# When the loads of one unit may start: a fixed time on the plan's clock, or the landing of a weight quarter

## The chip, the cores and the metric

The kernel runs on one core of one Trainium2 chip. The metric is the device time of one execution in microseconds (us). A core has five engines that run side by side, each through its own list of instructions in order: TensorE (PE in the profile; its weight loads are PEld), VectorE (DVE), ScalarE (ACT), GpSimd (POOL) and SyncE (SP). DMA transfers are started from SP's list (queue q1, "hardware_dynamic") or from POOL's (queue q0, "software_dynamic", which also casts fp32 to bf16 on the way) and run on 16 DMA engines that both queues share.

## What is computed

The inputs are q, k and v of shape (8 batches, 8 heads, 576 positions, 64), w_in (512 x 2048) and w_out (2048 x 512). First a retention layer, then a feed-forward layer over its 4608 rows of 512 (the reference, shortened):

```python
scores = scale * np.matmul(q, k.transpose(0, 1, 3, 2))
Dmat = np.where(rel >= 0, gamma[:, None, None] ** rel[None, :, :], 0.0)
attn = np.matmul(scores * Dmat[None], v)
x = attn.transpose(0, 2, 1, 3).reshape(B * S, H * D)
h = x @ w_in
g = np.where(h > 0.0, h, np.exp(np.minimum(h, 0.0)) - 1.0)
out = g @ w_out
```

rel is the distance of two positions, gamma one factor for each head.

## The kernel before

The retention is cut into items: a batch and one of its two stretches T of 256 positions, plus the items X and Y for the last 64 positions of four batches each. The six items of batches 0 to 2 are cut again, into two units of four heads each, so units 0 to 11 (u0 to u11): u0 and u1 make item 0, u2 and u3 item 1, u4 and u5 item 2. For each unit, three loads of 256 KB bring its q, k and v as fp32 from DRAM. DVE or POOL scale q and k by powers of gamma (line 522), ACT or POOL cast v (532), PE transposes q and k (554; from unit 6 on a DMA does it, 543), ACT or DVE copy them out of PSUM (560). Then PE makes scores, DVE masks them (888), PE makes the state and the values (line 265 is the helper of all matmuls, so they are told apart by tiles), DVE and others add up the state (823, 825, 841), and ACT or DVE write the result to xt, the input of the feed-forward layer (924).

The feed-forward layer goes by blocks. Blocks 0 to 13 are 256 rows wide, one item each; block 0 needs u0 and u1, block 1 u2 and u3, block 2 u4 and u5. F1 is the first layer: for 16 pieces of 128 columns of w_in, four matmuls of 128x256 each; two pieces share a PSUM bank, so F1 of such a block is eight groups of eight matmuls. After each group ACT takes the exponential (1041), ACT or DVE do a second step (1051, 1053, 1055), DVE makes g (1063, 1065). F2 is the second layer: each tile of 128 rows takes 16 matmuls of 128x512, four for each quarter of w_out. Block 0's F2 goes by pieces of w_out over its two tiles, all others go tile by tile.

The weights arrive in parts, started from POOL: w_in as wi0 and wi1 (one eighth each, 256 KB in bf16) and wi2, wi3, wi4 (a quarter each, 512 KB); w_out as wo0 to wo3 (a quarter each, 512 KB). The constants W_IN and W_OUT (lines 223, 224) name the parts.

The order in which each engine does all this is not written out by hand. A planner in the kernel (class Plan, lines 36 to 191) runs through the program as it is built, with a cost in microseconds for each step, ranks, slots of buffers, and a small model of the two DMA queues: ENTER and SW_ENTER are the times from issue to a transfer's first byte, the pair given as dma is its length and its number of packets, LEAVE the time from last byte to landing. At each moment each engine takes the ready step of lowest rank. What comes out is an order for each engine; on the chip there is no clock in it, only that order and the semaphores of true dependences. Where the plan shows PE a gap before 50 us, the code at lines 1183 to 1195 fills 0.8 of it with matmuls or transposes of a tile of zeros.

Four means shape the start of the order:

- AT (line 216) gives the earliest planned time at which a weight part may be issued on POOL (rank -1000, so first of what is ready).
- All loads are issued by SP in one chain, in the order in which `load` names them (378). For the items in VLATE (215) both units' v come after both units' q and k.
- HOLD (214) names loads that get an instruction on POOL ahead of them, planned not before the given time: a memset of one column of the load's tile (383). Because the load overwrites that tile, SP has to wait for the memset. All loads behind it in the chain are held with it.
- `cost_of` (933) and the numbers in `flush` (1019) tell the plan what PE's attention steps cost.

Of the kernel before, what the change touches and what calls it, by code (L numbers as in the profile page):

```python
# [191 lines left out]


ENTER, LEAVE = 1.25, 0.55
SW_ENTER = 4.2
TR_SP = 4.6
SLACK = 3.6
KV = 1.4
ISSUE = 0.65
JOINT = True  # L200
BD_ACT = 0.6
BD_POOL = 0.46
UB_POOL = 0.33
SCALED = 1.06
# [6 lines left out]
EARLY = 6  # L211
PE_TURN = 6
APART = (4, 5)
HOLD = {"ldq4": 14.4, "ldq5": 23.9, "ldv4": 30.1, "ldv6": 24.3}
VLATE = (0,)
AT = {"wi0": 6.9, "wi1": 10.0, "wi2": 7.2, "wi3": 11.0, "wi4": 17.7, "wo0": 18.0, "wo1": 21.0, "wo2": 21.3, "wo3": 27.5}
RANKS = {}
FREE = ("f", "e", "em", "g", "ot")
SURE = 3
# [13 lines left out]
def kernel(  # L233
# [28 lines left out]
    pin = tc.keep_in_program_order  # L262
# [113 lines left out]
    def load_part(name, dst, src, key, first, shape, cost=(0.9, 32)):  # L376
        def emit(op):
            pin(nc.sync.dma_start(dst(), src))  # L378

        hold = None  # L380
        if first and name in HOLD:
            def emit_h(op):
                pin(alu[op.eng].memset(tiles[key][:, 0, :1], 0.0))

            hold = add(f"hold{name}", {"POOL": 0.1}, [], emit_h, len(plan.ops) - 1000, take=[T("r", key, shape, FP32)])
            hold.early = HOLD[name]
            first = False
        op = add(name, {"SP": ISSUE}, [hold], emit, len(plan.ops), take=[T("r", key, shape, FP32)] if first else [],
                 use=[] if first else [key], dma=cost, after=chain.get(0))
        chain[0] = op  # L390
        return op

    def runs(src, b, hs, T):
        return src[b, hs, TB * T : TB * (T + 1), :].rearrange("h (p e) d -> p h (e d)", e=2)

    def load(it):
        n = it.n
        shape = [P, 2 * H, D]
        if it.units:
            for u, what in [(u, what) for u in it.units for what in "qkv"] if it.n not in VLATE else \  # L400
                    [(u, what) for u in it.units for what in "qk"] + [(u, "v") for u in it.units]:
                hs = slice(4 * u.w, 4 * u.w + 4)
                if what == "q":
                    u.ld = {}
                if what == "v":
                    u.ld["v"] = load_part(
                        f"ldv{u.n}", lambda hs=hs: tiles["rv", n].rearrange("p (h e) d -> p h (e d)", e=2)[:, hs],
                        runs(v, it.b, hs, it.T), ("rv", n), u.w == 0, shape, (0.89, 32))
                    continue
                i = "qk".index(what)  # L410
                u.ld[what] = load_part(
                    f"ld{what}{u.n}",
                    lambda u=u, i=i: tiles["rqk", u.n].rearrange("p (h e) d -> p h (e d)", e=2)[:, 4 * i : 4 * i + 4],
                    runs((q, k)[i], it.b, hs, it.T), ("rqk", u.n), i == 0, shape, (0.89 if u.n or not i else 1.5, 32))
            return
        it.ld = {}
        for name, src in (("v", v), ("k", k), ("q", q)):
            key = ("r" + name, n)
            it.ld[name] = []

            def part(tag, lo, n, s, b, t, key=key, src=src, name=name):
                def dst():
                    if s is None:
                        return tiles[key][lo : lo + n].rearrange("p (h e) d -> p h (e d)", e=2)
                    return tiles[key][lo : lo + n, s * H : (s + 1) * H]

                def rows_in():
                    if s is None:
                        return src[b, :, t : t + 2 * n, :].rearrange("h (p e) d -> p h (e d)", e=2)
                    return src[b, :, t : t + n, :].rearrange("h p d -> p h d")  # L430

                it.ld[name].append(load_part(f"ld{name}{tag}_{it.n}", dst, rows_in(), key, not it.ld[name], shape,
                                             ((1.8 if s is None else KV) * n / P, 64 * n // P)))

            if not it.tail:
                t = TB * it.T
                for s in (None,) if name == "q" else range(2):
                    part("" if s is None else s, 0, P, s, it.b, t + P * (s or 0))
            elif name == "q":
                for c in range(NC):  # L440
                    part(c, c * R, R, None, it.b + c, 2 * TB)
            else:
                for s in range(2):
                    for par in range(2):
                        part(2 * s + par, par * C, C, s, it.b + 2 * s + par, 2 * TB)
# [3 lines left out]
    def load_w_in(i):  # L449
        n0, n1 = W_IN[i]  # L450
        c = slice(n0 * 256, n1 * 256)

        def emit(op):
            pin(nc.gpsimd.dma_start(w_in_sb[:, :, c], moe_w_in[:, c].rearrange("(j p) n -> p j n", p=P)))

        op = add(f"wi{i}", {"POOL": 0.8}, [], emit, -1000, dma=(1.92 if n1 - n0 == 1 else 1.43 * (n1 - n0), 32 if n1 - n0 == 1 else 16 * (n1 - n0), SW_ENTER))
        op.slack = 0.4
        for ft in range(2 * n0, 2 * n1):
            w_in_ld[ft] = op

    def load_w_out(i):
        n0, n1 = W_OUT[i]

        def emit(op):
            pin(nc.gpsimd.dma_start(w_out_sb[:, 4 * n0 : 4 * n1],  # L465
                                    moe_w_out[n0 * 512 : n1 * 512, :].rearrange("(f p) n -> p f n", p=P)))

        op = add(f"wo{i}", {"POOL": 0.8}, [], emit, -1000, dma=(2.75 * (n1 - n0), 32 * (n1 - n0), SW_ENTER))
        op.slack = 0.4
        for ft in range(4 * n0, 4 * n1):  # L470
            w_out_ld[ft] = op
# [234 lines left out]
    def ustate_of(u, c):  # L706
        return ("s", u.b, 2 * u.T + c, u.w) if u.T + c else None
# [194 lines left out]
    def state_keys(it):  # L902
        return [s for s in ([ustate_of(it, c) for c in range(2)] if it.unit else [state_of(it, c) for c in range(NC)]) if s]
# [28 lines left out]

    def cost_of(it, parts):
        if it.unit:
            return (0.112 if state_keys(it) and "i" in parts else 0) + 0.24 * sum(p in parts for p in "sv") + \
                0.13 * ("t" in parts)
        t = 0.32 if "i" in parts else 0.0
        return t + 0.26 * sum(p in parts for p in "svt")

    def reserve(op, keys):  # L940
# [72 lines left out]
    def flush(it):  # L1013
        xkey = ("x", it)

        def emit(op):
            attend(it, None, xkey, None, 0)

        iv = add(f"iv{order_of.index(it)}", {"PE": (0.22 if it.unit and ustate_of(it, 0) is None else 0.45) + cost_of(it, "iv")}, inter_deps(it), emit, it.rank + 2, use=inter_uses(it))
        reserve(iv, pair_of(xkey))  # L1020
        put_x(it, xkey, iv)

# [207 lines left out]
```

## Time and profile before

| | before |
|---|---|
| median of 3 runs | 303.13 us |
| lowest and highest | 302.92 and 303.5 us |
| the profiled execution, its time | 302.48 us |
| the profiled execution, its span of instructions | 300.8 us |
| PE busy in the span | 294.7 us (98%) |
| DMA bytes moved | 50.41 MB |
| software queue q0, MB | 4.19 |

The page of the profile gives busy times by engine, slices of the span, DMA queues, the chain of work that ended last, and the costliest groups of instructions. Further views are answers to questions on the same trace: the timeline (start, length, engine, line, operation, output <- input, count, and in square brackets the idle time ahead and what ended it), the windows (busy time of each engine in a stretch, on request of one tile's instructions alone), the DMA view of a narrow window (each issue with its KB and its microseconds from issue to landing; the bytes of each queue in the window), and the chain in order of time. Matmul times in a row overlap: eight matmuls of 0.27 each start about 0.11 apart.

### The profile page before, as it was taken

The page shows a single profiled execution, that of the slowest core. Times are in us where ns is not written, and L with a number is a line of the kernel's source. Part 1 is how long each engine was busy: PE and PEld are TensorE (multiplying, and loading weights), DVE is VectorE, ACT ScalarE, POOL GpSimd, SP SyncE. Part 2 cuts the span into 40 slices and gives each one's busy share as a digit, 9 for nine tenths or more (in the row PEclk, how much of TensorE's full clock was granted, in tenths as well). Part 3 has the DMA queues.
Part 4 walks back from the last instruction along what each step waited for, and adds up shares of the span by engine and source line. Part 5 has one row for each costly group of instructions (what it writes and reads, how often), then busy time and mean ns, then how long its engine had stood idle before and what let it go on. Part 6 is the DMA issues. An engine that isn't in the chain of part 4 may idle for free.

```text
span 300.8 us, 9242 instructions
## 1 busy us (share of the span) xinstructions
PE 294.7 (98%) x3851; PEld 191.2 (64%) x3851; DVE 199.2 (66%) x379; ACT 164.5 (55%) x307; POOL 118.0 (39%) x195
## 2 busy tenths in 40 slices
PE   8999999999999999999999999999999999999995
PEld 5778746758665767677666576767676544444444
DVE  4876924957773777768687567678876667766500
ACT  3658823747653567457456356666666438644311
POOL 5856078654563516348066170835710000000000
PEclk9999999999999999999999999999999999999999
DMA  7999999999999985699999689757231000011131
GB/s 210 270 210 211 229 261 285 211 265 187 287 196 186 298 192 143 183 246 215 253 260 217 162 210 233 189 131 188 57 90 40 35 35 35 2 35 36 44 98 70
DMA packets 123498, 50.41 MB, mean 168 GB/s; under 512 B 83392, under 2 KB 118976, under 8 KB 123456
## 3 DMA queue, kind: packets, MB, share of 16 engines
q1 hardware_dynamic: 118704, 45.63, 64.1%
q0 software_dynamic: 4752, 4.19, 8.6%
q8 instruction: 30, 0.49, 0.7%
q14 instruction: 12, 0.10, 0.1%
HBM read 36.70 MB, written 9.44 MB: 153 GB/s over the span
## 4 chain that ended last, share of the span: by engine, by line
PE 90%; DMA 6%; POOL 2%; issue 0%; DVE 0%; ACT 0%; SPq 0%; ACTq 0%; POOLq 0%
PE f L265 88%; DMA r<-in_k_dram 4%; DMA r<-in_v_dram 3%; PE f L1191 1%; PE f L554 1%; POOL st L522 0%; POOL w_out_sb L465 0%; POOL vn L532 0%; POOL mask L494 0%; POOL pos_i L486 0%; ACT ot L1102 0%; SPq L378 0%; POOL s L841 0%; DVE mid L825 0%; POOL pos_i L489 0%
## 5 line engine op out<-in xcount | busy, mean ns | idle before, releaser
L265 PE MATMUL f<-w_out_sb,g 128*128 128x512 bf16 (+1 forms) x592 | 139.9, 374 | 0.0
L265 PE MATMUL f<-xt,w_in_sb 128*128 128x256 bf16 (+1 forms) x1024 | 139.6, 286 | 0.0
L1041 ACT ACTIVATE e<-f 128x512 f32<-128x512 f32 x144 | 85.6, 597 | 71.9 <-PE f L265 68.1
L265 PEld LDWEIGHTS <-w_in_sb 128*128 128x128 bf16 x1024 | 99.2, 98 | 35.5
L265 PEld LDWEIGHTS <-g 128*128 128x128 bf16 x592 | 56.5, 98 | 52.3
L1055 DVE TENSOR_SCALAR em<-e 128x512 bf16<-128x512 f32 x84 | 42.0, 502 | 40.1 <-ACT e L1041 39.7
L1065 DVE SCALAR_TENSOR_TENSOR g<-f,em 128x512 bf16<-128x512 f32 x84 | 57.0, 688 | 4.8
L1063 DVE SCALAR_TENSOR_TENSOR g<-e,f 128x512 bf16<-128x512 f32 x60 | 40.2, 683 | 10.1 <-ACT f L1051 9.1
L579 POOL CAST kv<-r 128x512 bf16<-128x512 f32 x24 | 14.4, 622 | 59.2 <-issue 57.4
L1102 ACT COPY ot<-f 128x512 f32<-128x512 f32 (+1 forms) x37 | 21.3, 575 | 27.0 <-PE f L265 26.5
L1051 ACT ACTIVATE f<-f 128x512 f32<-128x512 f32 x57 | 33.3, 591 | 0.0
L924 ACT CAST xt<-f 128x512 bf16<-128x512 f32 (+1 forms) x39 | 21.7, 611 | 18.0 <-PE f L265 17.8
L599 POOL TENSOR_TENSOR kv<-r,gk 128x512 bf16<-128x512 f32 x24 | 25.1, 1052 | 5.0 <-DMA r<-in_k_dram 5.0
L599 POOL TENSOR_TENSOR kv<-r,gq 128x512 bf16<-128x512 f32 x24 | 26.1, 1106 | 1.4 <-DMA r<-in_q_dram 1.4
L892 DVE TENSOR_TENSOR pt<-f,mask 128x512 bf16<-128x512 f32 x24 | 15.4, 683 | 9.4 <-PE f L265 9.4
L888 DVE TENSOR_TENSOR pt<-f,mask_u 128x512 bf16<-128x512 f32 x24 | 15.5, 682 | 3.7 <-PE f L265 3.7
L522 POOL TENSOR_TENSOR st<-r,gk 128x256 bf16<-128x256 f32 x21 | 13.1, 640 | 6.9 <-DMA r<-in_k_dram 6.9
L877 POOL CAST bd<-S 128x256 bf16<-128x256 f32 x29 | 11.5, 422 | 9.6 <-DVE S L865 5.9
L865 DVE TENSOR_TENSOR S<-f,S 128x256 f32<-128x256 f32 x30 | 12.6, 421 | 1.9
L522 POOL TENSOR_TENSOR st<-r,gq 128x256 bf16<-128x256 f32 x19 | 11.9, 643 | 1.6 <-DMA r<-in_q_dram 1.2
L265 PE MATMUL f<-T 64*64 64x64 bf16 (+1 forms) x576 | 10.5, 202 | 0.8 <-issue 0.8
L265 PEld LDWEIGHTS <-kv 64*64 64x64 bf16 x704 | 9.5, 104 | 0.1
(64 smaller groups left out, 144.1 us busy)
## 6 DMA issues: line engine op xcount, KB each, us to landing
r<-in_k_dram SPq DMA_DIRECT2D x32, 256.0 KB, 4.6
r<-in_v_dram SPq DMA_DIRECT2D x32, 256.0 KB, 4.9
out_dram<-ot SPq DMA_DIRECT2D x31, 256.0 KB, 2.6
r<-in_q_dram SPq DMA_DIRECT2D x10, 512.0 KB, 5.1
r<-in_q_dram SPq DMA_DIRECT2D x12, 256.0 KB, 5.1
w_out_sb<-in_moe_w_out_dram POOLq DMA_DIRECT2D x4, 512.0 KB, 13.0
w_in_sb<-in_moe_w_in_dram POOLq DMA_DIRECT2D x3, 512.0 KB, 12.1
out_dram<-ot SPq DMA_DIRECT2D x10, 128.0 KB, 2.3
```

Of the source, the lines that this page charges most:

```text
L265: return pin(nc.tensor.matmul(*a, **kw))
L522: pin(alu[op.eng].tensor_tensor(tiles[key][:, i, e].rearrange("p (y x) d -> p x y d", y=2), raw.rearrange("p (x y) d -> p x y d", y=2), g, ...
L599: pin(alu[op.eng].tensor_tensor(tiles[nkey][:, 2 * i + j].rearrange("p (y x d) -> p x y d", y=2, x=HP), raw.rearrange("p (x y) d -> p x y ...
L888: pin(nc.vector.tensor_tensor(pt, src.rearrange("p (h n) -> p h n", h=2), mask_u.rearrange("p k e r -> p (k e r)").unsqueeze(1).to_broadca ...
L892: pin(nc.vector.tensor_tensor(pt.rearrange("p h s n -> p (h s) n"), src.rearrange("p (h n) -> p h n", n=C), mask.rearrange("p e r -> p (e ...
L924: pin(copy[op.eng](dst, src))
L1041: pin(nc.scalar.activation(tiles[ekey], tiles[hkey], AF.Exp))
L1051: pin(nc.scalar.activation(ph, ph, AF.Relu))
L1055: pin(alu[op.eng].tensor_scalar_add(em, e, -1.0))
L1063: pin(nc.vector.scalar_tensor_tensor(g, e, -1.0, ph, ALU.add, ALU.min))
L1065: pin(nc.vector.scalar_tensor_tensor(g, ph, 0.0, tiles[mkey], ALU.max, ALU.min))
L1102: pin(copy[op.eng](tiles[okey][:, :width], tiles[pkey][:, :width]))
```

## The change

Only constants and the way of holding change. First, ldq4 (q of unit 4) alone keeps a hold, and it is no longer a planned time: HOLD now gives it a number of a part of w_out. The instruction ahead of the load is a copy of one column of that part of w_out_sb into the load's tile, on POOL, planned behind the landing of wo1. The loads ldq5, ldv4 and ldv6 lose their holds. Second, VLATE also takes item 1, so its loads go q, k of u2, q, k of u3, then v of both. Third, the times in AT: wi0 is planned later (8.5 for 6.9), wi1 sooner, wi2 later, wi4 and all of w_out sooner. Fourth, the plan's figures: SW_ENTER 3.2 for 4.2; a unit's load 0.84 for 0.89 (the first k 1.4 for 1.5); a part of w_in 1.65 or 1.3 per 256 columns for 1.92 or 1.43; a quarter of w_out 2.6 for 2.75; PE's costs of inter-chunk steps.

```diff
-SW_ENTER = 4.2
+SW_ENTER = 3.2
...
+WI, WI1, LD = 1.3, 1.65, 0.84
...
-HOLD = {"ldq4": 14.4, "ldq5": 23.9, "ldv4": 30.1, "ldv6": 24.3}
-VLATE = (0,)
-AT = {"wi0": 6.9, "wi1": 10.0, "wi2": 7.2, "wi3": 11.0, "wi4": 17.7, "wo0": 18.0, "wo1": 21.0, "wo2": 21.3, "wo3": 27.5}
+HOLD = {"ldq4": 1}
+VLATE = (0, 1)
+AT = {"wi0": 8.5, "wi1": 9.1, "wi2": 8.7, "wi3": 11.8, "wi4": 15.0, "wo0": 15.9, "wo1": 18.0, "wo2": 18.9, "wo3": 25.0}
...
         if first and name in HOLD:
+            behind = HOLD[name]
+
             def emit_h(op):
-                pin(alu[op.eng].memset(tiles[key][:, 0, :1], 0.0))
+                one = tiles[key][:, 0, :1]
+                if isinstance(behind, int):
+                    pin(copy[op.eng](one, w_out_sb[:, 4 * W_OUT[behind][0], :1]))
+                else:
+                    pin(alu[op.eng].memset(one, 0.0))
 
             hold = add(f"hold{name}", {"POOL": 0.1}, [], emit_h, len(plan.ops) - 1000, take=[T("r", key, shape, FP32)])
-            hold.early = HOLD[name]
+            if isinstance(behind, int):
+                holds.append((hold, f"wo{behind}"))
+            else:
+                hold.early = behind
             first = False
...
-                        runs(v, it.b, hs, it.T), ("rv", n), u.w == 0, shape, (0.89, 32))
+                        runs(v, it.b, hs, it.T), ("rv", n), u.w == 0, shape, (LD, 32))
...
-                    runs((q, k)[i], it.b, hs, it.T), ("rqk", u.n), i == 0, shape, (0.89 if u.n or not i else 1.5, 32))
+                    runs((q, k)[i], it.b, hs, it.T), ("rqk", u.n), i == 0, shape, (LD if u.n or not i else 1.4, 32))
...
-        op = add(f"wi{i}", {"POOL": 0.8}, [], emit, -1000, dma=(1.92 if n1 - n0 == 1 else 1.43 * (n1 - n0), 32 if n1 - n0 == 1 else 16 * (n1 - n0), SW_ENTER))
+        op = add(f"wi{i}", {"POOL": 0.8}, [], emit, -1000, dma=(WI1 if n1 - n0 == 1 else WI * (n1 - n0), 32 if n1 - n0 == 1 else 16 * (n1 - n0), SW_ENTER))
...
-        op = add(f"wo{i}", {"POOL": 0.8}, [], emit, -1000, dma=(2.75 * (n1 - n0), 32 * (n1 - n0), SW_ENTER))
+        op = add(f"wo{i}", {"POOL": 0.8}, [], emit, -1000, dma=(2 * WI * (n1 - n0), 32 * (n1 - n0), SW_ENTER))
...
-            return (0.112 if state_keys(it) and "i" in parts else 0) + 0.24 * sum(p in parts for p in "sv") + \
+            return (0.056 if state_keys(it) and "i" in parts else 0) + 0.24 * sum(p in parts for p in "sv") + \
                 0.13 * ("t" in parts)
-        t = 0.32 if "i" in parts else 0.0
+        t = 0.07 * len(state_keys(it)) if "i" in parts else 0.0
...
-        iv = add(f"iv{order_of.index(it)}", {"PE": (0.22 if it.unit and ustate_of(it, 0) is None else 0.45) + cost_of(it, "iv")}, inter_deps(it), emit, it.rank + 2, use=inter_uses(it))
+        iv = add(f"iv{order_of.index(it)}", {"PE": (0.28 if it.unit and ustate_of(it, 0) is None else 0.5) + cost_of(it, "iv")}, inter_deps(it), emit, it.rank + 2, use=inter_uses(it))
```

The list `holds` was there before, empty: at line 1164 each of its pairs gives the hold a dependence on the named weight part.

## The prediction

> **What bounds the kernel now.** I read the page first: span, engines, and the chain that ended last.
>
> ```profile
> span 300.8 us, 9242 instructions
> PE 294.7 (98%) x3851; PEld 191.2 (64%) x3851; DVE 199.2 (66%) x379; ACT 164.5 (55%) x307; POOL 118.0 (39%) x195
> PE 90%; DMA 6%; POOL 2%; issue 0%; DVE 0%; ACT 0%; SPq 0%; ACTq 0%; POOLq 0%
> ```
>
> PE is busy 98% of the span and is 90% of the chain. So the end moves only if PE does its real work sooner, and "busy" has to be split into real work and the zero matmuls that only fill planned gaps. The next two answers are the windows view kept to one tile each (window, its length, PE busy and count): first the tile of zeros, then w_in_sb, which is the first layer, F1.
>
> ```profile
> 14.00:18.00 4.00, 0.93 (x14) 0.68 (x14) 0.00 (x0) 1.00 1.28 204
> 18.00:22.00 4.00, 1.54 (x22) 1.17 (x22) 0.00 (x0) 1.00 1.21 215
> 22.00:26.00 4.00, 0.39 (x4) 0.31 (x4) 0.00 (x0) 1.00 1.21 217
> ```
>
> ```profile
> 14.00:18.00 4.00, 1.04 (x8) 0.74 (x8) 0.81 (x1) 1.00 1.28 204
> 18.00:22.00 4.00, 2.08 (x16) 1.44 (x16) 0.00 (x0) 1.00 1.21 215
> 22.00:26.00 4.00, 3.75 (x32) 3.00 (x33) 0.00 (x0) 1.00 1.21 217
> ```
>
> The columns are window, length, busy time and count of PE and of its weight loads, a third engine (DVE, then POOL), clock, DMA share and GB/s. From 14 to 22 us PE runs 36 matmuls of zeros, from 22 to 26 only four. F1 gets 24 matmuls in those eight microseconds and 32 in the next four. So PE can still win between 14 and 23 us; behind that it has real work nearly all the time. The timeline of PE there and behind, and one row of ACT, the last write of block 1's input:
>
> ```profile
> 15.98 1.04 PE L265 MATMUL f<-xt,w_in_sb 128*128 128x256 bf16 x8
> ...
> 17.61 0.39 PE L265 MATMUL f<-pt,vn 64*64 64x128 bf16 x16
> ...
> 22.13 1.05 PE L265 MATMUL f<-xt,w_in_sb 128*128 128x256 bf16 x8
> 22.43 0.46 ACT L924 CAST xt<-f 128x256 bf16<-128x256 f32 x1
> 23.23 1.91 PE L265 MATMUL f<-xt,w_in_sb 128*128 128x256 bf16 x16
> 28.85 6.29 PE L265 MATMUL f<-xt,w_in_sb 128*128 128x256 bf16 x56
> 34.98 3.62 PE L265 MATMUL f<-w_out_sb,g 128*128 128x512 bf16 x16
> 38.97 0.32 PE L265 MATMUL f<-vn,st 64*64 64x64 bf16 x16 [0.38 <-POOL vn L532]
> 49.99 5.40 PE L265 MATMUL f<-xt,w_in_sb 128*128 128x256 bf16 x48
> ```
>
> The 56 matmuls from 28.85 to 34.98 give 0.11 us each, 0.88 for a group of eight. The first four groups need 3.5 us and are spread from 15.98 to 23.0. From 23.23 PE is full to 34.98: 12 groups, 10.5 us, and the remaining 1.25 us are unit 4's transposes and scores. Then F2 (w_out) of block 0, the rest of units 4 and 5, and F1 of block 2 at 49.99. I use **two marks: the fifth F1 group (23.23) and block 2's F1 (49.99)**.
>
> What PE waits for until 23 is transfers. DMA issues, each from a narrow window (KB written, us to landing), in the order first two w_in pieces, v of unit 3, second quarter of w_out (wo1), last quarter (wo3), v of unit 5; then their issue times:
>
> ```profile
> w_in_sb<-in_moe_w_in_dram POOLq DMA_DIRECT2D x1, 256.0 KB, 7.5
> w_in_sb<-in_moe_w_in_dram POOLq DMA_DIRECT2D x1, 512.0 KB, 9.5
> r<-in_v_dram SPq DMA_DIRECT2D x1, 256.0 KB, 9.1
> w_out_sb<-in_moe_w_out_dram POOLq DMA_DIRECT2D x1, 512.0 KB, 12.2
> w_out_sb<-in_moe_w_out_dram POOLq DMA_DIRECT2D x1, 512.0 KB, 10.7
> r<-in_v_dram SPq DMA_DIRECT2D x1, 256.0 KB, 10.1
> ```
>
> ```profile
> 7.93 1.68 POOL L454 DMA_DIRECT2D w_in_sb<-in_moe_w_in_dram  x2
> 8.72 0.69 SPq L378 DMA_DIRECT2D r<-in_v_dram  x1
> 14.93 1.18 POOL L522 TENSOR_TENSOR st<-r,gk 128x256 bf16<-128x256 f32 x2 [0.49 <-DMA r<-in_k_dram]
> 21.04 1.48 POOL L465 DMA_DIRECT2D w_out_sb<-in_moe_w_out_dram  x2
> 29.29 0.80 POOL L465 DMA_DIRECT2D w_out_sb<-in_moe_w_out_dram  x1
> 30.13 0.16 POOL L383 MEMSET r<- 128x1 f32 x3
> 30.25 0.37 SPq L378 DMA_DIRECT2D r<-in_v_dram  x1
> 31.77 3.02 SPq L378 DMA_DIRECT2D r<-in_v_dram  x1
> ```
>
> So wi0 lands at 15.4, k of unit 3 at 14.9, v of unit 3 at 17.8, wo1 at 33.2, wo3 at 40.0, v of unit 5 at 41.9.
>
> **The change part by part.**
>
> *Unit 4's q and k leave the weights alone.* Today they are asked for at 14.5 and travel between the weights. Queue rows of 18 to 25 us and of 26 to 33 us (packets, MB, share):
>
> ```profile
> q1 hardware_dynamic: 989, 0.50, 35.0%
> q0 software_dynamic: 1061, 0.99, 84.7%
> ```
>
> ```profile
> q0 software_dynamic: 1428, 1.42, 122.7%
> ```
>
> In seven microseconds the weights move 0.99 MB beside these loads and 1.42 MB alone. The loss, 0.43 MB at 0.203 MB/us, is 2.1 us. Without it wo1 lands at 33.2 - 2.1 = 31.1; if the last two first loads, k and v of unit 3, also end before the weights start, 0.52 MB at the 341 GB/s of a row below, 1.5 us sooner still: 29.6. I take **30.6**. The bound on the other side is 33.2, nothing gained.
>
> *VLATE = (0, 1)* puts q and k of unit 3 one place further ahead, and puts v of unit 2 two places back. k is the longer way (scale 1.18, transposes, scores, masks). v of unit 2 is needed for values that today run at 17.61; its new place is that of today's k of unit 3, landing at 14.9, so it costs nothing; without that cover it costs what it lands late.
>
> *w_in later and in order.* The issues on POOL stay as many, at 0.74 to 0.84 each. The planned 8.5 instead of 6.9 for wi0 binds only if POOL has another instruction ahead; POOL runs in order and holds no clock. So wi0 is issued between 7.93 and about 9.5, and lands between 15.4 and 16. wi1 (256 KB) is behind it now, and wi2 (512 KB) third: 0.79 MB at 0.203 later, 19.3 to 20. With k of unit 3 at 12.5 to 14, and today's 8.0 from its landing (14.9) to the last write of block 1's input (22.9) less an F1 group of 0.9 between them, that write ends at 19.6 to 21; block 0's next groups can go ahead of block 1's. The first four groups then end at 20.0 at best, 21.2 at worst: fifth group at **20.6** instead of 23.23, 2.6 gained.
>
> *F1.* Twelve groups from 20.6 are 10.5 us: 31.1. The 1.25 us of unit 4 aren't between them any more; they come later.
>
> *F2.* wo1 is there at 30.6, wo0 0.52 MB earlier, at 28.0. Sixteen matmuls take 3.6, the third quarter 1.8: 36.5. wo3 follows wo1 by 6.8 today, with loads beside it; I take 6.3: 36.9, a stall of 0.4. From 34.98 to 49.99 PE needs 15.0 now; less the 0.4 of waiting at 38.97, plus 1.25, plus 0.4: 16.3. Block 2's F1 could start at 31.1 + 16.3 = 47.4.
>
> *The hold.* Four memsets of POOL (0.05 to 0.10) become one copy that waits for wo1. It reads bf16 and writes 128x1; bounds: the memset's 0.10 and the 0.59 of a scaling; I take 0.1. Behind it on POOL stand no weight issues (wo3 is planned at 25) and, soon, only unit 4's own scalings, so its wait delays nothing else. Behind it on SP stand all loads from unit 4 on: q, k, v of units 4 and 5 from 30.9. Today four loads asked from 30.25 end at 41.9, with wo3 at 40.0; wo3 is 3 us sooner, two loads are added (0.75 each at the row below): v of unit 5 at about 40.3.
>
> ```profile
> 6.00:10.00 4.00, 4.00 (x103) 3.27 (x102) 3.56 (x8) 1.91 (x5) 3.60 (x5) 1.00 1.13 341
> ```
>
> (Loads alone move 341 GB/s: 0.262 MB in 0.77 us.) Today block 2's F1 starts 8.1 after that landing, with other work of PE in between; the bare way is shorter, but POOL now has to scale unit 4 as well (four times 0.59) in the same stretch. I take 7.3: **47.6**. This is later than PE's 47.4 and decides.
>
> *Planner's costs* (SW_ENTER, LD, WI, iv, states) run nowhere; they move fillers and order. A filler is put only into 0.8 of a planned gap. Bounds: the 40 zeros behind 14 us all gone, by their busy times 0.93 + 1.54 + 0.39 = 2.9 won, but only where the data is there; or a few places worse, each like the 0.38 of the trace, 1.5 lost. I take 0, since zeros stand where PE waits.
>
> **Sum:** 49.99 - 47.6 = 2.4 us. One window from 50 to 280 us:
>
> ```profile
> 50.00:280.00 230.00, 229.92 (x3105) 148.65 (x3104) 163.68 (x295) 132.90 (x242) 88.78 (x127) 1.00 0.70 161
> ```
>
> PE is full there, so the lead should reach the end. The profiled execution took 302.48 (span 300.8, 1.7 around it) and becomes 300.1; the median 303.13 is 0.65 above it: **300.7**.
>
> **The rivals.**
>
> *Lead kept whole* (0.15). No wait for wo3 or unit 5: first mark 20.0, and 3.3 to 3.8 gained: 299.5. For it: F2 of block 1 can fill in. Against: units 4 and 5 start from nothing at 31.
>
> *Order changes nothing* (0.11). The same bytes go over the same engines; then v of unit 5 lands at 41.9 whatever the order, PE works sooner and waits there: 303.1, within 0.5. Against it: the 0.50 and 0.99 MB of the mixed seven microseconds would take 1.5 + 4.9 = 6.4 apart. The Trainium skill, DMA: Bandwidth & Descriptors, section "Issuing engines are not separate DMA queues", says that transfers started by different engines end up on the same 16 DMA engines and interleave; by that alone nothing is won by asking in another order, and the time would stay 303.1. The trace agrees that they share, but shows too that what shares lands late together.
>
> *Unit 4 starves PE* (0.19), the slower side. All of unit 4 now hangs on wo1. Each microsecond by which wo1 lands after 30.6 moves q, k and v of units 4 and 5, and block 2's F1, by as much. It breaks even at wo1 = 33.0. If k of unit 4 takes as long as today (row of the chain: issue, us to landing) the first mark's gain is gone too:
>
> ```profile
> 14.88 11.22 DMA r<-in_k_dram
> ```
>
> k asked for at 31.4 then lands at 42.6, four loads behind it at 0.4 each end at 44.2, and block 2 starts at 51.5, with PE idle before: 1.5 lost, 304.6, and each microsecond of wo1 adds one. For it: such latencies occur whenever weights are under way. Against: only wo2 and wo3 are left then.
>
> *The change does not do what it says* (0.05). wi0 is still issued at 7.93 behind the same instruction, the last loads still collide, and the new order places a few waits in 20 to 50: gain 0 to 1, or loss 1: about 303.
>
> **How the numbers follow.** Forecast 0.50 (its own range 299.9 to 302.3), lead whole 0.15, no change 0.11, starved 0.19, not done 0.05 (split: a third each way). 0.2% is 0.6 us, about what a measurement of this kernel can tell from no change. Faster: 0.50 + 0.15 + 0.02 = 0.67; same 0.11 + 0.02 = 0.13; slower 0.20. The range goes from 299.2 (all of 3.9) to 304.6 (starved at its price).
>
> **What would show it.** Right: zeros behind 14 us fall from 40 to under 25, by PE's count; the fifth F1 group starts by 21.2; F1 of blocks 0 and 1 ends by 32; wo1 lands by 31; q of unit 4 is asked for right behind it; block 2's F1 starts by 48. Wrong: wo1 after 32.5; a wait of PE on POOL or DMA of over 1 us between 36 and 50; k of unit 4 needing 10 us or more; new waits of PE behind 50 us, which today has none.

## The result and the profile after

| | before | after |
|---|---|---|
| median, lowest to highest | 303.31 us, 302.92 to 303.75 (6 runs) | 300.0 us, 299.2 to 300.54 (6 runs) |
| ratio after to before, 95% interval | | 0.9888 (0.9867 to 0.9908) |
| the profiled execution, its time | 302.48 us | 299.65 us |

The changed kernel is faster by 1.1%, some 3.4 us (the interval is 2.8 to 4.0). Here and below the times in us are medians of all executions of a kernel, and the ratios leave out executions that were some per cent longer at a lower granted clock. The two profiled executions differ by 302.48 - 299.65 = 2.83 us. Line numbers moved by one near the top and by ten further down: the matmul helper is now L266, the scalings L532, the casts of v L542, the transposes L564, the write of the feed-forward input L934, the loads L379, the weight issues L464 and L475.

Span, engines and the chain of the changed kernel, from its page:

```profile
span 297.9 us, 9155 instructions
PE 288.2 (97%) x3786; PEld 187.9 (63%) x3825; DVE 200.5 (67%) x378; ACT 163.7 (55%) x306; POOL 118.7 (40%) x194
PE 95%; DMA 1%; issue 1%; DVE 1%; SPq 0%; POOL 0%; ACT 0%; ACTq 0%
```

DMA, 6% of the chain before, is 1% now, and PE is 95% of it. The windows of the stretch that the prediction singled out, first for the tile of zeros, then for w_in_sb (window, length, PE busy and count, weight loads, a third engine, clock, DMA share, GB/s):

```profile
14.00:18.00 4.00, 0.53 (x8) 0.27 (x8) 0.00 (x0) 1.00 1.32 204
18.00:22.00 4.00, 0.54 (x7) 0.28 (x7) 0.00 (x0) 1.00 1.24 207
22.00:26.00 4.00, 0.00 (x0) 0.00 (x0) 0.00 (x0) 1.00 1.25 208
```

```profile
14.00:18.00 4.00, 1.05 (x8) 0.70 (x8) 0.80 (x1) 1.00 1.32 204
18.00:22.00 4.00, 2.77 (x24) 2.30 (x25) 0.00 (x0) 1.00 1.24 207
22.00:26.00 4.00, 4.00 (x39) 3.58 (x38) 0.00 (x0) 1.00 1.25 208
```

The zeros behind 14 us fell from 40 to 15, and none is left behind 22 us, where F1 now fills PE (4.00 of 4.00 us). The timeline of the changed kernel shows how that came about, up to block 2's F1:

```profile
8.56 0.61 POOL L542 CAST vn<-r 128x512 bf16<-128x512 f32 x1 [0.61 <-DMA r<-in_v_dram]
9.11 2.42 POOL L464 DMA_DIRECT2D w_in_sb<-in_moe_w_in_dram  x3
12.96 2.09 DVE L532 TENSOR_TENSOR st<-r,gq 128x256 bf16<-128x256 f32 x1
13.00 0.63 POOL L542 CAST vn<-r 128x512 bf16<-128x512 f32 x1
13.58 0.62 POOL L532 TENSOR_TENSOR st<-r,gq 128x256 bf16<-128x256 f32 x1
14.15 0.61 POOL L532 TENSOR_TENSOR st<-r,gk 128x256 bf16<-128x256 f32 x1
14.43 0.62 ACT L542 CAST vn<-r 128x512 bf16<-128x512 f32 x1 [0.67 <-DMA r<-in_v_dram]
15.11 0.40 PE L564 MATMUL f<-ident,st 128*128 128x128 bf16 x4 [0.78 <-DVE st L532]
16.37 1.05 PE L266 MATMUL f<-xt,w_in_sb 128*128 128x256 bf16 x8
18.36 1.05 PE L266 MATMUL f<-xt,w_in_sb 128*128 128x256 bf16 x8
20.28 12.39 PE L266 MATMUL f<-xt,w_in_sb 128*128 128x256 bf16 x112
20.45 0.45 ACT L934 CAST xt<-f 128x256 bf16<-128x256 f32 x1
29.88 0.19 POOL L388 CAST r<-w_out_sb 128x1 f32<-128x1 bf16 x1 [7.65 <-DMA w_out_sb<-in_moe_w_out_dram]
30.09 0.37 SPq L379 DMA_DIRECT2D r<-in_q_dram  x1
32.50 5.78 PE L266 MATMUL f<-w_out_sb,g 128*128 128x512 bf16 x25
47.51 4.75 PE L266 MATMUL f<-xt,w_in_sb 128*128 128x256 bf16 x42
```

Two F1 groups come singly at 16.37 and 18.36. From 20.28 the other 14 groups (112 matmuls) run without a break, and F2 follows at 32.50, 2.48 us sooner than before (34.98). Block 2's F1 starts at 47.51, again 2.48 sooner (49.99). The copy behind wo1 runs at 29.88, and 0.2 later unit 4's q is asked for. Three answers of the DMA view (KB, us from issue to landing): the third part of w_in (wi2, issued at 10.8), wo1, then k of unit 4:

```profile
w_in_sb<-in_moe_w_in_dram POOLq DMA_DIRECT2D x1, 512.0 KB, 8.8
```

```profile
w_out_sb<-in_moe_w_out_dram POOLq DMA_DIRECT2D x1, 512.0 KB, 11.7
```

```profile
r<-in_k_dram SPq DMA_DIRECT2D x1, 256.0 KB, 6.0
```

So wi2 lands at 19.6 and wo1 at 29.7, and k of unit 4 needs 6.0 us instead of 11.2. The list of what PE waits for now, over the whole span, has five rows. The one that matters for F1 (us in total, times, longest):

```profile
PE f L564 <- DVE st L532: 1.3, 2, 0.8
```

The others are 1.4 us without a named cause, the zero tile's first write (1.3), a cast of v (0.4) and a scaling on POOL (0.2). The 1.4 is probably no wait: this trace holds 3786 matmuls for 3825 weight loads, so records are missing, and a run with the same order of work and 3825 of both (held behind wo0, below) has no such row. None of the five is on a transfer. That alone is no change, for the list of before has none either: there zeros kept PE busy while the data came.

### The profile page after: what moved, and what is told of

Same layout as the page of the kernel before. It is cut to its first block, busy times and chain, and to the rows that moved or that the text cites. A ratio compares the mean times of both kernels' runs of the same rounds, so it can differ in the third digit from the quotient of the medians.

```text
span 297.9 us, 9155 instructions
## 1 busy us (share of the span) xinstructions
PE 288.2 (97%) x3786; PEld 187.9 (63%) x3825; DVE 200.5 (67%) x378; ACT 163.7 (55%) x306; POOL 118.7 (40%) x194
## 4 chain that ended last, share of the span: by engine, by line
PE 95%; DMA 1%; issue 1%; DVE 1%; SPq 0%; POOL 0%; ACT 0%; ACTq 0%
PE f L266 94%; DMA r<-in_q_dram 1%; PE f L564 1%; DVE st L532 1%; SPq L379 0%; POOL st L532 0%; PE f L1201 0%; ACT ot L1112 0%; DVE T L570 0%; ACTq L1112 0%
## 5 line engine op out<-in xcount | busy, mean ns | idle before, releaser
L266 PE MATMUL f<-xt,w_in_sb 128*128 128x256 bf16 (+1 forms) x1022 | 138.2, 286 | 0.1
L266 PE MATMUL f<-w_out_sb,g 128*128 128x512 bf16 (+1 forms) x555 | 133.6, 373 | 2.9 <-issue 1.4
L266 PEld LDWEIGHTS <-w_in_sb 128*128 128x128 bf16 x1024 | 99.3, 98 | 35.5
L266 PEld LDWEIGHTS <-g 128*128 128x128 bf16 x592 | 56.5, 98 | 52.6
L1065 DVE TENSOR_SCALAR em<-e 128x512 bf16<-128x512 f32 x79 | 40.9, 520 | 39.8 <-ACT e L1051 39.4
L1075 DVE SCALAR_TENSOR_TENSOR g<-f,em 128x512 bf16<-128x512 f32 x79 | 53.6, 688 | 4.4
L1073 DVE SCALAR_TENSOR_TENSOR g<-e,f 128x512 bf16<-128x512 f32 x65 | 43.5, 683 | 12.2 <-ACT f L1061 11.1
L1061 ACT ACTIVATE f<-f 128x512 f32<-128x512 f32 x60 | 35.5, 595 | 0.0
L1112 ACT COPY ot<-f 128x512 f32<-128x512 f32 (+1 forms) x35 | 20.1, 574 | 27.8 <-PE f L266 27.4
L934 ACT CAST xt<-f 128x512 bf16<-128x512 f32 (+1 forms) x43 | 23.0, 596 | 22.2 <-PE f L266 22.2
L609 POOL TENSOR_TENSOR kv<-r,gq 128x512 bf16<-128x512 f32 x24 | 26.8, 1138 | 0.0
L887 POOL CAST bd<-S 128x256 bf16<-128x256 f32 x30 | 11.4, 407 | 13.3 <-ACT S L873 6.7
L532 POOL TENSOR_TENSOR st<-r,gq 128x256 bf16<-128x256 f32 x19 | 12.0, 639 | 7.1 <-DMA r<-in_q_dram 6.5
L532 POOL TENSOR_TENSOR st<-r,gk 128x256 bf16<-128x256 f32 x19 | 11.9, 644 | 1.8 <-DMA r<-in_k_dram 1.8
L266 PE MATMUL f<-T 64*64 64x64 bf16 (+1 forms) x576 | 10.4, 202 | 0.0
L266 PEld LDWEIGHTS <-kv 64*64 64x64 bf16 x704 | 9.2, 104 | 0.0
```

Of the source, the lines that this page charges most:

```text
L266: return pin(nc.tensor.matmul(*a, **kw))
L532: pin(alu[op.eng].tensor_tensor(tiles[key][:, i, e].rearrange("p (y x) d -> p x y d", y=2), raw.rearrange("p (x y) d -> p x y d", y=2), g, ...
L609: pin(alu[op.eng].tensor_tensor(tiles[nkey][:, 2 * i + j].rearrange("p (y x d) -> p x y d", y=2, x=HP), raw.rearrange("p (x y) d -> p x y ...
L934: pin(copy[op.eng](dst, src))
L1061: pin(nc.scalar.activation(ph, ph, AF.Relu))
L1065: pin(alu[op.eng].tensor_scalar_add(em, e, -1.0))
```

## The experiments

My theory was the prediction's: the hold keeps unit 4 out of the weights' way, and the order of the first transfers brings F1 forward. What stayed open was which of the change's parts carry the gain, and whether the loads behind wo1 set block 2's F1. Each experiment is the changed kernel with one edit, unless its text says otherwise; the ratios are to the kernel before, on the same chip. For comparison, the changed kernel's is 0.9888.

### Must the hold be an event, and which one?

**A planned time again, but late.**

```diff
-HOLD = {"ldq4": 1}
+HOLD = {"ldq4": 29.6}
```

> The changed kernel, with a memset planned at 29.6 us ahead of q of unit 4 in place of the copy that waits for wo1. Theory (the landing has to be waited for): POOL has no clock and nothing before this memset from about 22 us on, so it runs at 22 to 23, q of unit 4 is asked for at once and six loads travel between the weights; wo1 lands at 31.5 to 33 and not at 29.8, wo3 at 38 or later, and the time is 301 to 302. Rival (event and planned time are worth the same, since the plan is calibrated): q is asked for at 29 to 30.5 and the time stays at 300.0, within 0.5.

Measured: 302.04 us, ratio 0.9949 (0.993 to 0.9967). This kernel's instructions stand in the same order as the changed kernel's on every engine, except for the one memset in the copy's place. The memset in its timeline, the DMA view of unit 4's k, and its one wait of PE on a transfer:

```profile
22.33 0.10 POOL L390 MEMSET r<- 128x1 f32 x1
```

```profile
r<-in_k_dram SPq DMA_DIRECT2D x1, 256.0 KB, 11.4
```

```profile
PE f L266 <- DMA w_out_sb<-in_moe_w_out_dram: 1.5, 1, 1.5
```

The memset was planned at 29.6 and ran at 22.33, as soon as POOL reached it; unit 4's q was asked for at 22.45. k of unit 4 took 11.4 us between the weights, and F2 stood 1.5 us waiting for a quarter of w_out. So the planned time did not hold the load; the event does.

**The four old holds in the changed kernel.**

```diff
-HOLD = {"ldq4": 1}
+HOLD = {"ldq4": 14.4, "ldq5": 23.9, "ldv4": 30.1, "ldv6": 24.3}
```

> The changed kernel with the four old holds at their planned times. Theory (q and k of unit 4 among the weights cost them about 2 us): asked for at 14 to 15, wo1 lands at 31.5 to 32, block 2's F1 starts at 48.5 to 49.5, the time is 301 to 302. Rival (the gain is that of the first loads' order, of w_in and of the figures, and the hold is by the way): block 2's F1 at 47.5 to 48 and a time of 300.0 to 300.4.

Measured: 301.8 us, ratio 0.9952 (0.9934 to 0.9971). Unit 4's q was asked for at 15.58. In its timeline unit 4's transposes stand inside F1 again, the first of them at 26.21, and F2 waits for a quarter of w_out:

```profile
26.21 0.39 PE L564 MATMUL f<-ident,st 128*128 128x128 bf16 x4
40.54 1.46 PE L266 MATMUL f<-w_out_sb,g 128*128 128x512 bf16 x6 [0.84 <-DMA w_out_sb<-in_moe_w_out_dram]
```

**One quarter sooner.**

```diff
-HOLD = {"ldq4": 1}
+HOLD = {"ldq4": 0}
```

> The changed kernel, held behind wo0, so q of unit 4 is asked for 2.6 us sooner, beside wo1 to wo3. Theory (loads set block 2's F1, but weights that share lose what the loads win): v of unit 5 lands at most 1.5 sooner, wo3 1 to 2 later, F2 of block 0 waits for it, and the time is 299.5 to 300.5. Rival (PE's work alone decides): 300.0, with nothing lost or won; a third way, the weights decide: slower by 0.5 to 1.5.

Measured: 299.76 us, ratio 0.9893 (0.9871 to 0.9914). The copy ran at 28.02, and block 2's F1 started at 47.46.

**One quarter later.** This one decides the step on which the predicted time rested: if the loads behind the hold set block 2's F1, a hold 3 us later must cost most of 3 us.

```diff
-HOLD = {"ldq4": 1}
+HOLD = {"ldq4": 2}
```

> The changed kernel, held behind wo2 instead of wo1, so q of unit 4 is asked for some 2.5 us later. Theory (the loads of units 4 and 5 set block 2's F1, as the prediction had it with 47.6 against PE's 47.4): block 2's F1 starts 1.5 to 2.5 later, at 49 to 50, and the time is 301.5 to 302.5. Rival (PE's own work sets it, the loads have slack): at most 0.5 lost, 300.0 to 300.5.

Measured: 300.11 us, ratio 0.9901 (0.9883 to 0.992). The copy and block 2's F1 in its timeline:

```profile
32.90 0.19 POOL L388 CAST r<-w_out_sb 128x1 f32<-128x1 bf16 x1 [11.08 <-DMA w_out_sb<-in_moe_w_out_dram]
47.95 5.40 PE L266 MATMUL f<-xt,w_in_sb 128*128 128x256 bf16 x48
```

q of unit 4 was asked for 3.0 us later (33.11 for 30.09), v of unit 5, the last of the six loads, landed 1.7 later (41.2 for 39.5), and block 2's F1 started 0.44 later. My theory fell here: these loads have slack, and PE's own work sets that mark. Between 28 and 33 us the place of the hold is flat within what the runs can tell. At 22 or 15 us it costs about 2. In those two profiles 0.7 to 1.0 of it is a late v of unit 3 (below), which the hold at 22 us can't have caused, since it came behind it; 1.5 to 1.7 at block 2's F1 is left for the hold.

### What does the hold do alone?

The kernel before, with nothing but the event:

```diff
-HOLD = {"ldq4": 14.4, "ldq5": 23.9, "ldv4": 30.1, "ldv6": 24.3}
+HOLD = {"ldq4": 1}
```

> The kernel before with one part of the change alone: the hold of q of unit 4 behind wo1's landing, the three other holds gone; VLATE, AT and all figures of the plan as before. Theory (the hold is worth some 1.7 of the 3.3 us, by the changed kernel with the old holds at 301.8): wo1 lands at 31 or sooner, F1 of blocks 0 and 1 ends 1 to 2 sooner than before, the time is 301.0 to 302.0. Rival (without the earlier first loads the hold wins nothing, since F1 still starts late): 302.7 to 303.3. Second rival (the hold is all): 300.0 to 300.5.

Measured: 301.66 us, ratio 0.996 (0.9942 to 0.9978). Its timeline:

```profile
23.43 10.64 PE L266 MATMUL f<-xt,w_in_sb 128*128 128x256 bf16 x96
33.91 5.78 PE L266 MATMUL f<-w_out_sb,g 128*128 128x512 bf16 x26
48.72 5.40 PE L266 MATMUL f<-xt,w_in_sb 128*128 128x256 bf16 x48
```

The fifth F1 group is at 23.43, no sooner than before (23.23). The 1.07 us by which F2 starts sooner (33.91 for 34.98) come from unit 4's transposes and scores, which no longer stand between F1's groups. They are done inside F2 instead, and there they cost nothing: block 2's F1 is 1.27 sooner (48.72 for 49.99). wo1, issued at 20.73 for 21.04, landed at 30.2 for 33.2, so most of what the change wins on this quarter is the hold's. Together with the run with the old holds, the parts nearly add up: the hold alone takes 0.4% off, the rest of the change without the hold 0.48%, both 1.12%, each with an uncertainty of some 0.2.

### Which of the other parts carry the rest?

Six runs put parts of it back, first one at a time.

**VLATE:**

```diff
-VLATE = (0, 1)
+VLATE = (0,)
```

> The changed kernel with VLATE as before, so v of unit 2 is loaded ahead of q and k of unit 3. Theory (k of unit 3 is the longer way): unit 3's chain is 0.5 to 1 later, the fifth F1 group too, but from there weights and PE's own work decide: 300.0 to 300.7. Rival (the order of the first loads is what the gain comes from): 301 or more.

**PE's plan costs:**

```diff
-            return (0.056 if state_keys(it) and "i" in parts else 0) + ...
+            return (0.112 if state_keys(it) and "i" in parts else 0) + ...
-        t = 0.07 * len(state_keys(it)) if "i" in parts else 0.0
+        t = 0.32 if "i" in parts else 0.0
-        iv = add(..., {"PE": (0.28 if it.unit and ustate_of(it, 0) is None else 0.5) + ...
+        iv = add(..., {"PE": (0.22 if it.unit and ustate_of(it, 0) is None else 0.45) + ...
```

> The changed kernel with PE's costs of the plan alone as before (states and values alone: 0.112, 0.32, 0.22, 0.45); the figures of the DMA queues stay changed. Theory (all figures back cost 3.9 us because the plan then expects transfers at other times than the chip has them): these four are not transfers, so at most 0.6 from the changed kernel, 299.6 to 300.6. Rival (PE's costs set the order that matters): 302 to 304.

**AT:**

```diff
-AT = {"wi0": 8.5, "wi1": 9.1, "wi2": 8.7, "wi3": 11.8, "wi4": 15.0, "wo0": 15.9, "wo1": 18.0, "wo2": 18.9, "wo3": 25.0}
+AT = {"wi0": 6.9, "wi1": 10.0, "wi2": 7.2, "wi3": 11.0, "wi4": 17.7, "wo0": 18.0, "wo1": 21.0, "wo2": 21.3, "wo3": 27.5}
```

> The changed kernel with the issue times of the weights as before (AT). Theory (weights asked for while the first loads still run cost those loads as much as they win): wi0 issued at about 8, v of unit 3 lands 1 to 3 later than in the changed kernel, the fifth F1 group 0.5 to 1.5 later, and wo0 to wo3 asked for later but still in time for their queue: 300.4 to 301.2. Rival (only the hold matters, the weights' queue is full anyway): 300.0, within 0.4.

**All of the plan's figures,** those of PE as above and those of the queues:

```diff
-SW_ENTER = 3.2
+SW_ENTER = 4.2
-WI, WI1, LD = 1.3, 1.65, 0.84
+WI, WI1, LD = 1.43, 1.92, 0.89
-... (LD if u.n or not i else 1.4, 32))
+... (LD if u.n or not i else 1.5, 32))
-... dma=(2 * WI * (n1 - n0), 32 * (n1 - n0), SW_ENTER))
+... dma=(2.75 * (n1 - n0), 32 * (n1 - n0), SW_ENTER))
```

> The changed kernel with the plan's figures as before (SW_ENTER, the lengths of loads and weight parts, PE's cost of states and of values alone); HOLD, VLATE and AT as changed. Theory (figures run nowhere and move only order and zeros): within 0.5 of the changed kernel, 299.6 to 300.6. Rival (with wrong lengths the plan puts steps on POOL and DVE in an order that waits on the chip): 300.8 to 302, with waits of PE on POOL, DVE or ACT between 20 and 50 us that the changed kernel does not have.

**The queues' figures alone,** the diff above without PE's:

> The changed kernel with the figures of the DMA queues alone as before (SW_ENTER 4.2, the lengths of loads and weight parts). Theory: this alone brings the loss of all figures back, 302.5 to 304.5, with the first layer's seventh group at 22 to 23 us where the changed kernel has it at 20.3, and waits of PE on POOL or DVE. Rival: 299.8 to 300.6, the loss then being due to PE's costs.

**VLATE and PE's plan costs together,** their two diffs above, so that three parts of the change are left:

> The changed kernel with VLATE and PE's costs of the plan as before, so only the hold behind wo1, AT and the figures of the DMA queues are changed. Theory (these three carry the gain and need one another, the two others are by the way): 299.5 to 300.3, block 2's F1 at 47 to 47.6. Rival (a little of the gain is VLATE's and the costs', each being hidden by the other when it is undone alone): 300.5 to 301.5.

What the six measured, with three starts from each kernel's timeline:

| put back | us | ratio (95%) | wi0 issued | v of unit 3 cast | third F1 group |
|---|---|---|---|---|---|
| nothing | 300.0 | 0.9888 (0.9867 to 0.9908) | 9.11 | 14.43 | 20.28 |
| VLATE | 299.82 | 0.99 (0.988 to 0.9921) | 8.86 | 14.25 | 19.90 |
| PE's plan costs | 299.8 | 0.9889 (0.9875 to 0.9903) | 9.47 | 14.77 | 20.05 |
| VLATE and PE's plan costs | 300.93 | 0.9918 (0.9893 to 0.9944) | 9.22 | 14.36 | 20.29 |
| queue figures | 305.16 | 1.004 (1.0012 to 1.0068) | 8.31 | 16.74 | 21.97 |
| queue figures and PE's plan costs | 303.89 | 1.002 (0.9993 to 1.0046) | 8.08 | 17.21 | 22.75 |
| AT | 302.61 | 0.999 (0.997 to 1.001) | 8.32 | 18.35 | 20.20 |

The profiled execution with the queue figures back is the shortest of its 12 (302.11 us; the longest took 310.57), so its columns show the smaller part of that loss. The last three columns show what goes with the planner's figures on the chip. Where wi0 is issued at 8.86 or later, v of unit 3, the last of the first loads, is cast by 14.8 and the third F1 group starts at about 20. Where wi0 is issued at 8.32 or sooner, that load is cast 2 to 4 us later. In the first group SP has issued v of unit 3 0.4 to 0.5 us ahead of wi0 (8.7 in the changed kernel), in the second some 0.8 behind it (9.1 with AT back). With the queue figures back the third group is 1.7 and 2.5 us late; with AT back it is in time, but from there F1 comes in pieces and the fifth group starts at 23.67. No run moves wi0 alone, so this is a pattern over profiles, one for each kernel, and not a shown cause. What sets the time of wi0 is neither the AT time nor a figure by itself, but what the plan puts ahead of it on POOL (planned not before 8.5, it ran at 8.31 with the queue figures back). There the timeline has both of the first two casts of v on ACT, and POOL free for the weights:

```profile
8.19 1.35 ACT L542 CAST vn<-r 128x512 bf16<-128x512 f32 x2 [2.39 <-DMA r<-in_v_dram]
8.31 2.42 POOL L464 DMA_DIRECT2D w_in_sb<-in_moe_w_in_dram  x3
16.74 0.62 ACT L542 CAST vn<-r 128x512 bf16<-128x512 f32 x1 [2.43 <-DMA r<-in_v_dram]
17.41 0.32 PE L266 MATMUL f<-vn,st 64*64 64x64 bf16 x16 [0.86 <-ACT vn L542]
```

In the changed kernel POOL casts the second of the two at 8.56, and wi0 has to wait until 9.11. In no profile was that load in time without the delay, but the delay doesn't always do: in the profiles with the planned hold and with the old holds wi0 went at 9.17 and 9.45, and v of unit 3 was still cast only at 16.43 and 16.11. Since the first of these runs the changed kernel's instructions in the changed kernel's order up to 22 us, this is a spread between executions, and about 1 us of that profile's distance (its F1 runs from 21.25) with it.

The table also says that the queue figures and AT only work together. By the ratios, undoing AT loses 1.0% and undoing the queue figures 1.5%, each more than undoing everything but the hold (0.7%). The run with three parts, which was to show that VLATE and PE's costs can go, came out 0.9 us worse than the changed kernel, with overlapping intervals. In its timeline unit 4's transposes stand sooner in F2, and PE meets them before POOL has scaled:

```profile
39.56 0.28 PE L564 MATMUL f<-ident,st 128*128 128x128 bf16 x2 [0.25 <-POOL st L532]
```

Such waits add up to 1.0 us there, against 0.2 in the changed kernel. Block 2's F1 starts at 48.53, 1.02 late, which is the loss. Either part put back alone costs nothing, so what matters seems to be the order that comes out, not the part.

### Is it DVE's scaling that holds the third group?

In the changed kernel one scaling on DVE took 2.09 us at 12.96, beside three instructions of POOL, and PE waited for it. The experiment does units 2 and 3's scalings on DVE only, and their casts on ACT only:

```diff
-cq[i, e] = add(..., {"POOL": 0.62, "DVE": 0.5} if n < 4 else ...
+cq[i, e] = add(..., {"DVE": 0.5} if n in (2, 3) else {"POOL": 0.62, "DVE": 0.5} if n < 4 else ...
-u.laid = [add(f"cv{n}", {"ACT": 0.62, "POOL": 0.65, ...} if n < 4 else ...
+u.laid = [add(f"cv{n}", {"ACT": 0.62} if n in (2, 3) else {"ACT": 0.62, "POOL": 0.65, ...} if n < 4 else ...
```

> The changed kernel with all scalings of q and k of units 2 and 3 on DVE and the casts of their v on ACT, none on POOL. Theory (a scaling on DVE that takes 0.42 alone took 2.09 at 12.96 us because POOL ran three instructions at that time): each takes 0.41 to 0.50, PE's wait for a scaling at 15 us (0.8) goes, block 1's input is written 0.5 to 1 sooner than at 20.9, and the time is 299.3 to 300.0, little gained since wi2 lands at 19.6. Rival (DVE took 2.09 for a reason of its own): single scalings still take 1 to 2 us, unit 3 is later by the work that POOL did, and the time is 300.3 to 301.5.

Measured: 301.53 us, ratio 0.9947 (0.9927 to 0.9967). The profiled execution is the longest of the six (305.66 us), so of its timeline the stretch up to block 1's F1 is read here:

```profile
13.60 0.75 DVE L532 TENSOR_TENSOR st<-r,gq 128x256 bf16<-128x256 f32 x2
16.43 0.41 DVE L532 TENSOR_TENSOR st<-r,gk 128x256 bf16<-128x256 f32 x1
20.37 1.92 PE L266 MATMUL f<-xt,w_in_sb 128*128 128x256 bf16 x16 [0.45 <-DMA w_in_sb<-in_moe_w_in_dram]
```

With POOL out of the way each scaling takes 0.4. That part of the theory held, and the rival's reason fell. But the third group starts at 20.37, no sooner than in the changed kernel, and here PE waits for its part of w_in. So the scaling alone does not hold the third group: in the changed kernel too wi2 lands only at 19.6, 0.7 ahead of it. The gain did not come: the plan now puts unit 3's last scaling behind other work of DVE, at 16.43, block 1's input is complete at 23.9 instead of 20.9, and the fifth group starts at 23.04, 1.0 later than in the changed kernel. The kernel is 1.5 us slower than the changed one.

## Why the prediction was right or wrong

Direction and size were right: 300.7 foretold, 300.0 measured, inside the range. Of the 0.7, some 0.3 are the starting point (the profiled execution before lay 0.65 under its median, the one after 0.35) and 0.43 the gain itself: 2.83 by the profiles, 2.4 foretold. But the 2.4 were reached by steps of which two were off in opposite directions, and one was wrong. F1's end came 1.4 later than foretold and F2 took 1.3 less; that the two cancel at 47.5 is luck. Of the six signs that were to show it right, four came; the fifth F1 group by 21.2 (22.05) and F1's end by 32 (32.5) did not.

- **wo1 at 30.6: right.** Issued at 18.01 and 11.7 us under way, it landed at 29.7. With a load between the weights a quarter of w_out held up F2, as the two runs with planned times show.
- **wi0 between 7.93 and 9.5, bound only by an instruction ahead of it on POOL: right,** 9.11 behind the cast at 8.56. That so much goes with this instruction I did not see.
- **The first mark, 20.6: mis-sized.** The third group starts at 20.28, and at 0.885 a group (12.39 us for 14) the fifth at 22.05: 1.2 us gained, not 2.6. I had four groups done by then; only two were. My own time for wi2 (19.3 to 20) rules out four: the third and fourth group of block 0 need that part, and block 1's first two need an input that I had at 19.6 at the soonest, so the fifth group could not start before 19.3 + 2 x 0.885 = 21.1. I let "block 0's next groups go ahead" without asking for their weights. wi2 landed at 19.6, inside the range. The other 0.7 us up to 20.28 PE spends on the end of unit 3, for which it waited 0.78 on a scaling that took 2.09 us on DVE; I had the 1.18 of POOL for two in mind. The last write of block 1's input ends at 20.9, inside the foretold 19.6 to 21.
- **F1's end, 31.1: wrong by the same 1.4;** it was 32.5. That unit 4's 1.25 us leave F1 was right, and the hold alone shows it apart.
- **F2 to block 2's F1, 16.3 us: mis-sized.** It took 15.0, as before, though unit 4's work was added. Counted by weight loads, from 34.9 to 49.9 before and from 32.4 to 47.2 after, both have 52 of F2. The groups of the transposes and of the scores there, first before, then after (busy, mean ns, idle time in front):

```profile
L554 PEld LDWEIGHTS <-st 128*128 128x128 bf16 x8 | 0.6, 98 | 0.5
L265 PEld LDWEIGHTS <-T 64*64 64x64 bf16 x16 | 0.3, 106 | 0.4 <-DVE mid L825 0.4
```

```profile
L564 PEld LDWEIGHTS <-st 128*128 128x128 bf16 x16 | 1.2, 98 | 0.9
L266 PEld LDWEIGHTS <-T 64*64 64x64 bf16 x32 | 0.6, 107 | 0.4 <-DVE mid L833 0.4
```

  Eight transposes and 16 score matmuls more fit into the same 15.0 us. The stall for wo3, foretold at 0.4, didn't come: wo3 landed at 35.2, not 36.9. And of the 1.25 that I charged for unit 4 some 0.35 was a wait, which didn't move along. In the timeline of before, the second pair of transposes starts 0.46 behind the first, where a pair takes 0.11:

```profile
26.95 0.28 PE L554 MATMUL f<-ident,st 128*128 128x128 bf16 x2
27.41 0.28 PE L554 MATMUL f<-ident,st 128*128 128x128 bf16 x2 [0.19 <-POOL st L522]
```

  Where the remaining half microsecond came from is open.
- **"Later than PE's 47.4 and decides" (v of unit 5 plus 7.3): wrong.** The number, 47.6, was met at 47.51, but by PE's own work. Loads asked for 3 us later moved it by 0.44, and v of unit 5, foretold at 40.3, landed at 39.5.
- **The planner's figures at 0, bounds 2.9 won and 1.5 lost: the term that was missing.** Undoing the queue figures alone loses 1.5%, some 4.6 us. They "run nowhere", as I wrote, but they choose which engine casts, and so when the weights start. The bound was set by gaps in which PE waits. What the runs showed in its place is, in the shortest execution, a load some 2 us late and 2.5 us lost at the end, and in longer ones a lower clock of PE (last section). How the loss divides between the two was not measured. AT, for which the prediction had another term, loses 1.0% when put back; there the load is 4 us late, but PE's waits on scalings of DVE are longer too (2.4 us for 1.3), so the load isn't shown to be the only cause.
- **VLATE and the hold copy at next to nothing: right** (299.82 with VLATE back; the copy took 0.19).
- **The rivals.** "Lead kept whole" was right in its condition, for PE waited neither for wo3 nor for unit 5, and wrong in its first mark (20.0); its 299.5 is nearer to the measured 300.0 than the forecast. "Unit 4 starves PE" fell, even with a hold 3 us later. "Order changes nothing" fell: a load between the weights costs 1.5 to 2 us, and the kernels with AT or the queue figures back, whose weights start 0.8 sooner, are slower by 2.6 us and more. The sentence of the Trainium skill, DMA: Bandwidth & Descriptors, section "Issuing engines are not separate DMA queues", stands as far as it goes. k of unit 4 took 11.4 us among the weights and 6.0 behind wo1, so the engines are shared; what the order changes is which of the sharers is late.
- **The lead reaches the end: right,** 2.48 at 47.5 and 2.83 at the end. The 0.35 more arise behind block 2 and were not traced.

## What to carry to other kernels

A time in a plan is no time on the chip: an instruction in an in-order queue runs when its queue reaches it, so a transfer that must not start early has to hang on an event, such as the landing of the transfer that it would disturb. Once it does, its exact place mattered little here (28 to 33 us were alike), whereas the figures of the plan mattered through the order that came out of them, so look at the one instruction ahead of the first weight as well as at the figure. And a mark that two bounds reach within 0.2 us doesn't tell which one decides; delay one of them by 3 us and see.

## What the runs showed of the hardware

**DVE blocked by POOL.** A scaling on DVE (128x256, two inputs) takes 0.41 alone and took 2.09 beside three instructions of POOL, ending 15.05, 0.29 behind the last of them (14.15 + 0.61). Longer cases stand in two other timelines, first with units 2 and 3's scalings on DVE, then with all figures back:

```profile
49.23 5.19 DVE L1065 TENSOR_SCALAR em<-e 128x512 bf16<-128x512 f32 x1 [2.08 <-ACT e L1051]
```

```profile
53.42 4.12 DVE L1065 TENSOR_SCALAR em<-e 128x512 bf16<-128x512 f32 x1 [2.02 <-ACT e L1051]
56.64 0.62 POOL L542 CAST vn<-r 128x512 bf16<-128x512 f32 x1
58.48 0.22 PE L266 MATMUL f<-vn,st 64*64 64x64 bf16 x2 [1.89 <-DVE g L1075]
```

The same step takes 0.52 on the mean of the changed kernel. In the first case it lasted until 54.42, 0.29 behind the last of eight instructions of POOL in a row. In the second it lasted until 57.54, 0.28 behind POOL's last cast, and PE stood 1.89 us. The Trainium skill, SBUF — State Buffer, section "Who interferes with whom", says that DVE and GpSimd share one pair of ports under an exclusive lock, among others when a DVE instruction has two inputs in SBUF as this scaling has, and that whoever comes second waits for the whole of the other's instruction. The trace agrees, for in all three cases DVE ended just behind POOL. It goes further in that DVE waited not for one instruction but for a row of them, whose records overlap (13.00 + 0.63 against 13.58), and in that at 12.96 its record starts 0.04 ahead of POOL's cast.

**A short stall halves the clock.** The granted clock in the second of these kernels, all figures back, in windows of 1 us (PE busy and count, weight loads, DVE, ACT, POOL, then the clock):

```profile
57.00:58.00 1.00, 0.00 (x0) 0.00 (x0) 0.90 (x2) 0.37 (x1) 0.26 (x1) 1.00 1.93 238
...
60.00:61.00 1.00, 1.00 (x6) 0.52 (x5) 1.00 (x3) 0.43 (x1) 1.00 (x3) 0.50 0.87 261
61.00:62.00 1.00, 1.00 (x6) 0.71 (x5) 1.00 (x3) 0.16 (x1) 1.00 (x3) 0.50 0.01 4
```

PE had nothing from 57 to 58, 0.59 us of work in the window before and 0.23 in the one behind, so it stood for some 2.2 us of three. From 60 to 63 us, when it was busy again, its clock was 0.50 (0.93 in the window before, 0.86 in the one behind), so the wait of 1.89 us cost about 1.7 more. The run with units 2 and 3's scalings on DVE shows the same: behind its step of 5.19 us PE was busy for 0.00, 0.56 and 0.07 of the windows from 54 to 57 us, and its clock was 0.50 from 58 to 60. The Trainium skill, TensorE: Matmul & The Clock Gate, section "Part 1: The HAM clock gate", puts the fall at an idle window of about 3.4 us; here 2.2 us, with a few matmuls in between, were enough. The twelve executions with all figures back fall into three groups by the mean granted clock: 302.3 to 302.8 us at 0.998 or more, 303.4 to 306.6 at 0.992 to 0.994, and 309.0 to 309.5 at 0.983. By the trace one such stretch takes 1.7 us of clock, 0.6% of the span, so 0.994 would be one and 0.983 three. That is an estimate; which waits start them in the longest executions no profile shows.
